# A fused attention and MoE kernel on one core: the last chunk's output in two halves, two clamps on POOL, and a new order of all operations

## Chip, cores, metric

The kernel runs on 1 core of a Trainium2 chip. The metric is the device time of one execution in microseconds. Engines: PE (matmul), DVE, ACT and POOL (elementwise work), SP (issues the DMA transfers).

## What is computed

Inputs are q, k, v of shape 4 x 8 x 768 x 64 (batch, head, position, head dimension) in f32, and two matrices, w_in (512 x 2048) and w_out (2048 x 512), in f64.

```python
k_sum = k.reshape(B, H, nb, 32, D).max(axis=3)        # 24 block summaries of k
v_sum = v.reshape(B, H, nb, 32, D).mean(axis=3)       # and of v
scores_l = scale * q @ k.T,  only where |i - j| < 16
scores_s = scale * q @ k_sum.T + log(32)
a = softmax over [scores_l, scores_s]
x = (a @ [v, v_sum]).reshape(3072, 512)
h = x @ w_in;  g = h * cos(h);  out = g @ w_out
```

## The kernel before

The 3072 rows are cut into 8 blocks of 384 rows (blk 0 to 7). Each block has two parts.

**Attention**, for four groups a, b, c, d of two heads each; a2 is group a of block 2. A group's steps: loads of q, k, v and of the summaries of v (`q k v m`, issued on SP), transposes on PE and copies into place (`tq tk cq ck`, from block 2 on `qt kt` on DVE), summaries of k (`ks`), masks and scores on PE (`ms sc`, lines 553 to 573), scores from PSUM to SBUF (`z`), maximum (`mx`, DVE), subtraction of it (`su`, POOL, line 593), exp (`ex`, ACT), sums (`sm`, DVE), reciprocal (`iv`, DVE), normalization (`nm`, POOL, line 617), transposes of the probabilities on PE and their copies (`tp cp`), the product with the values on PE (`va`, line 670), and its split into a high and a low fp32r part (`xh xl`, lines 350 and 356). `v0_0` to `v3_7` are the block sums of v (`l` load, `h` halve, `s` sum). `v0_0` holds heads 0 to 3 of batch 0, `v0_1` heads 4 to 7.

**The two products**, as 128 steps s0 to s127, each one 128-wide slice f of the 2048 columns for one block of rows. `up` (12 matmuls, line 714) gives h. `tu re si sq ga` make the gate (lines 724 to 741, ACT DVE ACT ACT DVE), `hi lo` split it (lines 350 to 356, on an engine that the order names). `dh dl` (9 matmuls, line 770) add it to three accumulators in PSUM, one for each chunk of 128 rows. At the end of a run the accumulators are copied (`ta`) and stored (`st`, SP). The runs: s0 to s5 are block 0 with slices 0 to 5, s6 to s21 block 1 with all 16, s22 to s31 block 0 with the other ten, and then one run of 16 for each of blocks 2 to 7.

**The weights** are turned from f64 words into a high and a low fp32r part on the chip, once for each slice w0 to w15: `l` (two loads of 512 KB each on SP, lines 371 and 375, into raw space that several slices share in turn; the space is given by `SLOTS`), `ab` (magnitude, ACT, line 388), `cl` (DVE, a clamp of a 128 x 1024 tile, line 393), `sh lb fb` (bits put together, DVE, lines 399 to 415), `hi` and `lo` (lines 423 and 426). s0 needs w0, s1 needs w1, and so on. So the first third of the kernel does three things at once: attention of blocks 0 and 1, the splitting of the weights, and the first steps.

Nothing in the order is decided by a scheduler: `ORDER` lists all operations as tokens, such as `w3.cl` or `s5.up.0` (the number is a PSUM bank), and every engine, SP among them, gets its own instructions in the order of that list and works through them in that order (lines 898 to 903). SP's loads go round eight semaphores; a load waits until the one eight places before it has landed. Waits between engines come from the data.

## Time and profile before

| | |
|---|---|
| median of 3 runs (lowest, highest) | 661.95 us (660.78, 662.87) |
| the profiled execution | 662.1 us |
| its span, first to last instruction | 660.2 us |
| mean granted clock of TensorE | 0.987 |
| busy: PE, DVE, ACT, POOL | 633.9, 451.1, 366.2, 214.6 us |
| moved by DMA | 72.68 MB |

In rows of the timeline the columns are start, length, engine, line, operation, output<-input, shape, count, and in brackets the idle time before and what ended it. SPq rows are issues of transfers. A window's row gives the busy time of PE, PEld, DVE, ACT and POOL with their counts, then the granted clock, the DMA engines' busy share and GB/s. A row of a group gives, behind the bar, the busy time and the mean length in ns, and then the idle time before.

### The profile page before, as it was taken

Reading aid. Unit: us, or ns where it says so; the run is one execution under the profiler, and the core shown is the slowest. Engines: PE = TensorE matmul, PEld = TensorE weight load, DVE = VectorE, ACT = ScalarE, POOL = GpSimd, SP = SyncE. Lnnn points to the kernel's source line nnn. Section 1 sums busy time; section 2 is a strip of 40 time slices with the busy share of each in tenths; the row PEclk is TensorE's granted clock in tenths of the full one; section 3 lists DMA queues with packets and bytes.
Section 4 is the critical chain, followed back from the end, with each engine's and each line's share of the span. In section 5 each row is a group of like instructions: output and inputs, shape, how many; then the busy total and the mean of one; then the engine's idle time right before and its main releaser. Section 6 shows DMA issues by size and latency. Waiting matters only on the chain.

```text
span 660.2 us, 13296 instructions
## 1 busy us (share of the span) xinstructions
PE 633.9 (96%) x5150; PEld 561.5 (85%) x5150; DVE 451.1 (68%) x792; ACT 366.2 (55%) x645; POOL 214.6 (33%) x217
## 2 busy tenths in 40 slices
PE   6569999999999999999999999999999999999997
PEld 4347889889888989898988988989898988989996
DVE  3998998988656676658786667577686564534433
ACT  3666968776663375546575663335545554443443
POOL 4674777754220242302333340012332132010001
PEclk9879999999999999999999999999999999999999
DMA  9898725443331443434553544423243424000001
GB/s 229 260 268 224 239 94 176 160 111 59 69 108 52 128 127 105 115 71 98 123 156 78 150 125 132 92 54 81 85 120 104 104 91 115 0 1 17 32 1 48
DMA packets 164647, 72.68 MB, mean 110 GB/s; under 512 B 134441, under 2 KB 153193, under 8 KB 164585
## 3 DMA queue, kind: packets, MB, share of 16 engines
q1 hardware_dynamic: 164584, 71.84, 40.6%
q8 instruction: 40, 0.66, 0.4%
q14 instruction: 23, 0.18, 0.1%
...
## 4 chain that ended last, share of the span: by engine, by line
PE 87%; SPq 4%; DMA 4%; ACT 2%; issue 1%; DVE 1%; POOL 1%; ACTq 0%
PE banks L770 40%; PE banks L714 39%; PE banks L569 4%; PE banks L670 3%; DMA late<-in_moe_w_out_dram 3%; SPq L456 1%; SPq L493 1%; SPq L477 1%; ACT stage L388 1%; ACT L732 0%; POOL w L356 0%; SPq L485 0%; PE banks L626 0%; ACT w L350 0%; SPq L254 0%
## 5 line engine op out<-in xcount | busy, mean ns | idle before, releaser
L714 PE MATMUL banks<-xh,w 128*128 128x384 f32 x1024 | 271.8, 337 | 1.1 <-ACT pt L350 0.7
L770 PE MATMUL banks<-w,gh 128*128 128x512 f32 x768 | 199.1, 394 | 0.0
L714 PEld LDWEIGHTS banks<-xh,w 128*128 128x128 f32 x1024 | 185.9, 188 | 3.9 <-ACT pt L350 0.9
L714 PE MATMUL banks<-xl,w 128*128 128x384 f32 x512 | 171.4, 335 | 0.0
L770 PEld LDWEIGHTS banks<-w,gh 128*128 128x128 f32 x768 | 142.0, 188 | 29.0
L356 POOL TENSOR_TENSOR gl<-t,gh 128x384 fp32r<-128x384 f32 x57 | 58.5, 1027 | 242.9 <-DVE gh L352 86.0
L724 ACT ACTIVATE t<-banks 128x384 int32<-128x384 f32 x128 | 62.2, 489 | 131.1 <-DVE gl L356 56.1
L727 DVE SCALAR_TENSOR_TENSOR t<-t,banks 128x384 f32<-128x384 int32 x128 | 69.5, 547 | 61.2 <-ACT t L724 60.7
L770 PE MATMUL banks<-w,gl 128*128 128x512 f32 x384 | 109.6, 393 | 0.0
L739 DVE SCALAR_TENSOR_TENSOR t<-t,banks 128x384 f32<-128x384 f32 x128 | 69.8, 547 | 45.4 <-ACT t L735 44.9
L732 ACT ACTIVATE t<-t 128x384 f32<-128x384 f32 x128 | 66.3, 523 | 60.1 <-DVE t L727 59.4
L714 PEld LDWEIGHTS banks<-xl,w 128*128 128x128 f32 x512 | 96.1, 188 | 1.7
L770 PEld LDWEIGHTS banks<-w,gl 128*128 128x128 f32 x384 | 71.3, 188 | 14.8 <-POOL gl L356 0.2
L593 POOL TENSOR_TENSOR sc<-sc,m 128x720 f32<-128x720 f32 x28 | 39.5, 1410 | 88.9 <-DVE m L588 83.8
L735 ACT ACTIVATE t<-t 128x384 f32<-128x384 f32 x128 | 65.9, 522 | 2.4
L617 POOL TENSOR_TENSOR sc<-sc,r 128x720 f32<-128x720 f32 x28 | 39.6, 1416 | 73.1 <-DVE r L614 70.2
L350 ACT CAST gh<-t 128x384 fp32r<-128x384 f32 x71 | 36.2, 510 | 41.3 <-PE banks L770 21.8
L356 DVE TENSOR_TENSOR gl<-t,gh 128x384 fp32r<-128x384 f32 x71 | 40.6, 573 | 19.6 <-PE banks L770 12.0
L356 POOL TENSOR_TENSOR w<-stage,w 128x1024 fp32r<-128x1024 f32 x15 | 36.7, 2448 | 14.7 <-ACT w L350 12.8
L569 PEld LDWEIGHTS banks<-kd,qd 64*64 64x64 f32 x1344 | 27.8, 133 | 9.6 <-issue 5.3
L580 DVE SCALAR_TENSOR_TENSOR sc<-banks,mask 128x360 f32<-128x360 f32 x48 | 24.7, 523 | 16.5 <-PE banks L569 16.3
L569 PE MATMUL banks<-kd,qd 64*64 64x96 f32 (+1 forms) x1344 | 30.9, 231 | 0.6 <-ACT qd L508 0.4
...
## 6 DMA issues: line engine op xcount, KB each, us to landing
...
```

The costliest lines, as they stand in the source:

```text
L350: eng.copy(out=out, in_=in_)
L356: eng.tensor_tensor(out=lo, in0=src, in1=hi.bitcast(F32), op=ALU.subtract)
L569: nc.tensor.matmul(out=self.sp[hh][s * QT : (s + 1) * QT, c, lo : lo + n], lhsT=self.qd[rows, t * QT : (t + 1) * QT], rhs=self.kd[rows, ke ...
L593: nc.gpsimd.tensor_tensor(out=self.sc, in0=self.sc, in1=self.m.unsqueeze(2).broadcast_to([P, U, NK]), op=ALU.subtract)
L617: nc.gpsimd.tensor_tensor(out=self.sc, in0=self.sc, in1=self.r.unsqueeze(2).broadcast_to([P, U, NK]), op=ALU.mult)
L714: nc.tensor.matmul(out=self.h, lhsT=w_of(name, self.f)[:, c * P : (c + 1) * P], rhs=x_of(self.blk, part, c), start=n == 0, stop=n == last,)
L724: nc.scalar.activation(out=self.t.bitcast(I32), in_=self.h, func=AF.Copy, scale=1.0 / TWO_PI)
L727: nc.vector.scalar_tensor_tensor(out=self.t, in0=self.t.bitcast(I32), scalar=-TWO_PI, in1=self.h, op0=ALU.mult, op1=ALU.add)
L732: nc.scalar.activation(out=self.t, in_=self.t, func=AF.Sin, scale=0.5)
L735: nc.scalar.activation(out=self.t, in_=self.t, func=AF.Square, scale=math.sqrt(2.0))
L739: nc.vector.scalar_tensor_tensor(out=self.t, in0=self.t, scalar=-1.0, in1=self.h, op0=ALU.add, op1=ALU.mult)
L770: nc.tensor.matmul(out=self.acc[i], lhsT=g[:, i * P : (i + 1) * P], rhs=w_of(name, self.f), start=self.first and n == 0, stop=self.last an ...
```

## The change

Three things are changed.

1. **The last chunk.** The third chunk of a block's last run was copied by one instruction of 512 columns and stored by one transfer of 256 KB. Now two instructions of 256 columns each copy it, on engines that the order names (`ta` and the new `tb`), and two transfers store the halves (`st` and the new `sb`). This concerns the chunk that is copied into the tile `last`, which is that of s127 only.
2. **The clamp** (`cl`) takes an engine from the order. w3 and w7 are clamped on POOL, the other 14 on DVE as before.
3. **The order.** All 2247 tokens stand in a new order, and there are two more (`s127.tb`, `s127.sb`). PSUM banks are given out differently, and some copies change their engine: of the steps' `hi`, 66 are on ACT (before 71) and 62 on DVE (57); of their `lo`, 66 on DVE (71) and 62 on POOL (57). The loads' spaces (`SLOTS`) and the runs stay.

```diff
-        def clamp(self):
+        def clamp(self, eng):
-            nc.vector.tensor_scalar(out=uf, in0=uf, scalar1=W_LO, scalar2=W_HI, op0=ALU.max, op1=ALU.min)
+            eng.tensor_scalar(out=uf, in0=uf, scalar1=W_LO, scalar2=W_HI, op0=ALU.max, op1=ALU.min)
...
-                t = xp.tile([P, 2, TB], F32R, name="last", tag="xh0%d" % (self.blk % 2))
-                self.o[i] = t.rearrange("p c n -> p (c n)")[:, :DM].bitcast(F32)
+                return self.take_half(i, 0, eng)
...
+        def take_half(self, i, h, eng):
+            if (i, 0) not in self.o:
+                t = xp.tile([P, 2, TB], F32R, name="last", tag="xh0%d" % (self.blk % 2)).rearrange("p c n -> p (c n)")
+                self.o[i, 0], self.o[i, 1] = (t[:, n * DM // 2 : (n + 1) * DM // 2].bitcast(F32) for n in range(2))
+            self.negative(eng, self.o[i, h], self.acc[i][:, h * DM // 2 : (h + 1) * DM // 2])
...
+        def store_half(self, i, h):
+            r0, c = self.blk * TB + i * P, slice(h * DM // 2, (h + 1) * DM // 2)
+            nc.sync.dma_start(out=out[r0 : r0 + P, c], in_=self.o[i, h])
...
 ORDER = """
-s127.lo.p s127.dh s127.dl s127.ta.1.1.a s127.ta.0.0.v s127.ta.2.a s127.st.1 s127.st.2 s127.st.0
+s127.lo.p s127.dh s127.dl s127.ta.2.a s127.ta.0.0.v s127.st.2 s127.tb.2.v s127.st.0 s127.ta.1.1.v s127.sb.2 s127.st.1
```

SP, from the load of w0 on (late_131 holds w0, late_125 w2, late_132 w1 and then w5; vn_103 belongs to a0, x_0_135 to c0; vs are the block sums of v, from v0_0 and v0_1). Before:

```order
L375 DMA late_131<-in_moe_w_out_dram 128x1024
L456 DMA late_130<-in_q_dram 128x3x64 x2
L477 DMA vn_103<-in_v_dram 96x5x64 x2
L485 DMA vn_103<-in_v_dram 80x2x64
L371 DMA late_125<-in_moe_w_in_dram 128x4x256
L375 DMA late_125<-in_moe_w_out_dram 128x1024
L493 DMA x_0_135<-vs_299 24x6x64 x2
L493 DMA vn_103<-vs_292 24x6x64 x2
L371 DMA late_132<-in_moe_w_in_dram 128x4x256
```

And now:

```order
L376 DMA late_131<-in_moe_w_out_dram 128x1024
L494 DMA x_0_135<-vs_297 24x6x64 x2
L372 DMA late_125<-in_moe_w_in_dram 128x4x256
L376 DMA late_125<-in_moe_w_out_dram 128x1024
L478 DMA x_0_135<-in_v_dram 96x5x64 x2
L486 DMA x_0_135<-in_v_dram 80x2x64
L494 DMA vn_103<-vs_290 24x6x64 x2
L478 DMA vn_103<-in_v_dram 96x5x64 x2
L486 DMA vn_103<-in_v_dram 80x2x64
L457 DMA late_130<-in_q_dram 128x3x64 x2
L372 DMA late_132<-in_moe_w_in_dram 128x4x256
```

The load of c1's q (late_130) has gone from the first place behind w0 to the last before w5, and the values of c0 have come ahead of a0's. Further down SP's list, w4.l stood behind a1.m, d1.m and a1.q and ahead of d0.v, c1.m, d1.q and b0.m; now it stands behind c1.m, d0.m, a1.q, d1.q, d0.v and b0.m, and ahead of b1.m, a1.m and d1.m. The loads that followed w8 in the order w7, v1_0, w9, w10, w6 (with others between) now follow as v1_0, w6, w9, w7, w10.

POOL, from w2's low part on (w_485 and w_483 are w2, w_552 and w_553 are w5; sc is a score tile of group b0 or a1). Before:

```order
L356 TENSOR_TENSOR w_485<-stage_480,w_485 128x1024
L593 TENSOR_TENSOR sc<-sc,m 128x6x120
L356 TENSOR_TENSOR w_552<-stage_520,w_552 128x1024
L617 TENSOR_TENSOR sc<-sc,r 128x6x120
L593 TENSOR_TENSOR sc<-sc,m 128x6x120
```

And now:

```order
L357 TENSOR_TENSOR w_483<-stage_465,w_483 128x1024
L594 TENSOR_TENSOR sc<-sc,m 128x6x120
L394 TENSOR_SCALAR stage_494<-stage_494 128x1024
L618 TENSOR_TENSOR sc<-sc,r 128x6x120
L594 TENSOR_TENSOR sc<-sc,m 128x6x120
L357 TENSOR_TENSOR w_553<-stage_522,w_553 128x1024
```

The clamp of w3 (L394) has come behind b0.su, and the low part of w5 has gone behind b0.nm and a1.su. The same place on DVE, with w3 as stage_501 (before) and stage_494 (now), and w4 as stage_585 and stage_587. Before:

```order
L415 SCALAR_TENSOR_TENSOR stage_520<-late_132,banks 128x1024
L393 TENSOR_SCALAR stage_501<-stage_501 128x1024
L609 TENSOR_REDUCE r<-sc 128x6
L399 TENSOR_SCALAR banks<-stage_501 128x1024
L614 RECIPROCAL r<-r 128x6
L407 SCALAR_TENSOR_TENSOR banks<-late_126,banks 128x1024
L356 TENSOR_TENSOR xl_0_588<-banks,xh_0_446 128x384
L588 TENSOR_REDUCE m<-sc 128x6
L393 TENSOR_SCALAR stage_585<-stage_585 128x1024
```

And now:

```order
L416 SCALAR_TENSOR_TENSOR stage_522<-late_132,banks 128x1024
L610 TENSOR_REDUCE r<-sc 128x6
L400 TENSOR_SCALAR banks<-stage_494 128x1024
L615 RECIPROCAL r<-r 128x6
L589 TENSOR_REDUCE m<-sc 128x6
L357 TENSOR_TENSOR xl_0_519<-banks,xh_0_500 128x384
L394 TENSOR_SCALAR stage_587<-stage_587 128x1024
L408 SCALAR_TENSOR_TENSOR banks<-late_126,banks 128x1024
```

w3's clamp is gone from DVE, a0's low part (xl_0_588 before) now stands earlier in the list than these rows, d0's low part (xl_0_519) has come ahead of w4's clamp, and w3's `lb` (L408) has gone behind it.

SP at the end of the program (stage tiles hold chunks 0 and 1, `last` chunk 2). Before:

```order
L810 DMA out_dram<-stage_6472 128x512
L810 DMA out_dram<-stage_6911 128x512
L810 DMA out_dram<-last 128x512
L810 DMA out_dram<-stage_6913 128x512
L929 UNCONDITIONAL_BRANCH
```

And now:

```order
L827 DMA out_dram<-stage_6552 128x512
L831 DMA out_dram<-last 128x256
L827 DMA out_dram<-stage_6915 128x512
L831 DMA out_dram<-last 128x256
L827 DMA out_dram<-stage_6920 128x512
L954 UNCONDITIONAL_BRANCH
```

The first row is an earlier block's store. Of s127's stores, chunk 1 was first, chunk 2 second and chunk 0 last; now they are the first half of chunk 2, chunk 0, the second half of chunk 2, chunk 1. On ACT the copies of chunks 1 and 2 are replaced by that of the first half; DVE copies chunk 0, the second half and then chunk 1.

319 lines of the change are left out of this document (166 added, 153 removed).

## The prediction

> **What bounds the kernel now.** I read the page first, then the busy time in windows, then the timeline of PE.
>
> ```profile
> PE 633.9 (96%) x5150; PEld 561.5 (85%) x5150; DVE 451.1 (68%) x792; ACT 366.2 (55%) x645; POOL 214.6 (33%) x217
> 80.00:90.00 10.00, 9.32 (x70) 7.84 (x69) 9.79 (x15) 9.78 (x17) 7.94 (x8) 1.00 0.17 45
> 300.00:400.00 100.00, 100.00 (x957) 88.79 (x956) 74.23 (x141) 63.05 (x103) 35.36 (x33) 1.00 0.49 122
> ```
>
> PE is busy 633.9 of 660.2 us, so 26.3 us are all that any order of the same matmuls could win. From 84 us to the last matmul there is no gap (the window 300:400 is full, at clock 1.00). What can move is therefore the first 84 us and the end. The rows of PE that matter at the start:
>
> ```profile
> 48.33 1.26 PE L670 MATMUL banks<-pt,x 120*64 120x64 f32 x24 [2.17 <-DMA x<-in_v_dram]
> 58.27 0.43 PE L714 MATMUL banks<-xh,w 128*128 128x384 f32 x1
> 66.94 1.09 PE L626 MATMUL banks<-ident,late 128*120 128x128 f32 x6 [0.49 <-POOL late L617]
> 68.42 0.44 PE L714 MATMUL banks<-xh,w 128*128 128x384 f32 x1 [0.39 <-ACT late L350]
> 83.15 0.44 PE L714 MATMUL banks<-xh,w 128*128 128x384 f32 x1 [0.68 <-ACT pt L350]
> 94.45 4.19 PE banks L714 x24
> ```
>
> 58.27 is s0.up, the first matmul of the two products, and needs the last x part of block 0 (b0.xl, on DVE). 94.45 (from the chain) is s6.up, where the first run is done. Between the two PE waits only 0.49 + 0.39 + 0.68 = 1.56 us. Before s0.up DVE is the limit:
>
> ```profile
> 17.16 1.38 DVE L259 TENSOR_TENSOR late<-late 96x1024 f32<-96x1024 f32 x1 [1.16 <-DMA late<-in_v_dram]
> 22.61 1.65 DVE L393 TENSOR_SCALAR stage<-stage 128x1024 f32<-128x1024 f32 x1 [0.37 <-ACT stage L388]
> 24.19 0.18 DVE L614 RECIPROCAL r<-r 128x6 f32<-128x6 f32 x1
> 44.73 0.72 DVE L393 TENSOR_SCALAR stage<-stage 128x1024 f32<-128x1024 f32 x1
> 45.78 0.91 DVE L609 TENSOR_REDUCE r<-sc 128x6 f32<-128x726 f32 x1 [0.32 <-ACT sc L606]
> 49.00 0.55 DVE L356 TENSOR_TENSOR xl<-banks,xh 128x384 fp32r<-128x384 f32 x1
> 51.17 1.26 DVE L393 TENSOR_SCALAR stage<-stage 128x1024 f32<-128x1024 f32 x1 [0.82 <-ACT stage L388]
> 57.57 0.56 DVE L356 TENSOR_TENSOR xl<-banks,xh 128x384 fp32r<-128x384 f32 x1
> ```
>
> In order: the halving of v0_0, w1.cl, a0.iv, w3.cl, b0.sm, a0.xl, w4.cl, b0.xl. From w1.cl on DVE runs almost without a break to b0.xl, which ends at 58.13, and s0.up follows 0.14 us later.
>
> **The start, term by term.** Every instruction up to s0.up is the same but for w3.cl, which goes to POOL.
>
> First, up to b0.sm. a0.sm and a0.iv go ahead: a0.sm now runs in the 1.16 us that DVE waits for v0_0, and a0.iv no longer stands behind w1.cl (0.18 us off that stretch). w1.cl itself took 1.65 us where w3.cl took 0.72; the difference is POOL's work beside it:
>
> ```profile
> 21.71 0.24 POOL L280 TENSOR_SCALAR vs<-vs 96x64 f32<-96x64 f32 x1
> 22.33 1.39 POOL L593 TENSOR_TENSOR late<-late,m 128x720 f32<-128x720 f32 x1 [0.39 <-DVE m L588]
> L297 POOL TENSOR_SCALAR_AFFINE_SELECT mask<-mask 64x384 f32<-64x384 f32 x2 | 1.0, 524 | 0.1
> L259 POOL TENSOR_TENSOR late<-late 96x1024 f32<-96x1024 f32 x1 | 2.4, 2353 | 0.0
> 44.94 0.81 ACT L606 ACTIVATE sc<-sc 128x720 f32<-128x720 f32 x1 [0.96 <-POOL sc L593]
> ```
>
> c0.su ends at 23.72, and w1.cl can only then go. With c0.mx earlier, c0.su starts when POOL is free, at 21.95, 0.4 us sooner; I take 0.3. So DVE is about 0.5 us ahead when it comes to b0.sm. w3.cl's 0.72 us ahead of b0.sm also goes, but the earlier a0.xl (0.55 us) takes most of its place, and b0.sm waits for b0.ex anyway (0.32 us now). b0.sm: 0.6 us earlier, at about 45.2.
>
> Then w3.sh, behind b0.sm, now waits for POOL's clamp. POOL can start it when b0.su is done, as ACT starts b0.ex; so it has b0.ex (0.81 us) and b0.sm (0.91 us), 1.7 us, before DVE waits. The trace has no clamp of this size on POOL. The nearest one-input row, 524 ns for 384 elements, gives 1024/384 × 0.524 = 1.4 us; the two-input row of 1024 elements gives 2.35 us. I take 1.4 (one input, like the clamp): no wait. At 2.35 it is 0.65 us. The Trainium skill, page "GPSIMD Engine Reference", section 3.1, puts a light one-input body at 1.03 cycles an element against some 2.5 for two inputs, which at its 1.2 GHz would be 0.9 us, an estimate from that page; by it the sum is that with no wait, by the two-input row the sum is 0.65 us more. No run yet shows it.
>
> From b0.sm to b0.xl. Before: 45.78 to 58.13, 12.35 us. Now a0.xl is out of it (0.5 us), and the wait of 0.82 us for w4.ab changes. ACT did w4.ab at 50.01, behind d0.xh, which waited for d0.va, which waited 2.17 us for d0.v. The loads of d0.v came behind w4.l and now stand ahead of it. What then comes last is w4's own load:
>
> ```profile
> 41.64 5.98 DMA late<-in_moe_w_out_dram
> 56.41 6.92 DMA late<-in_moe_w_out_dram
> 50.01 1.14 ACT L388 ACTIVATE stage<-late 128x1024 f32<-128x1024 f32 x1
> 17.58 3.30 SPq L456 DMA_DIRECT2D late<-in_q_dram  x2
> 71.51 1.14 ACT L388 ACTIVATE stage<-late 128x1024 f32<-128x1024 f32 x1 [0.74 <-DMA late<-in_moe_w_out_dram]
> ```
>
> w4 landed 5.98 us after its issue, at 47.62. Five more issues stand ahead of it now (c1.m, d1.q, d0.v and b0.m against a1.m and d1.m), at about 0.8 us each 4 us; against that SP's slow issues between 17 and 27 us fall away in part (c1.q alone took 3.30 us for two), since SP then waits for v0_1 with less in flight. I take the difference as 1 us, so w4 lands at 48.6 and w4.ab ends at 49.8, against 51.15. w4.cl then may meet a1.su on POOL as it met it before (1.26 us, not 0.72). From w4.cl's end to b0.xl's end DVE has the same work but for d0.xl, done before, against w3.lb, done after. I take 1.1 us less than the 12.35: the 0.5 of a0.xl and 0.6 of the wait.
>
> Start: 0.6 + 1.1 = **1.7 us earlier at s0.up** (56.6). Bounds: 0, if w4 lands 7 us after a later issue; 2.6, if DVE nowhere waits.
>
> Second, s0.up to s6.up, 36.18 us now. c1.nm goes ahead of b1.su, so the 0.49 us at 66.94 and the 0.39 at 68.42 should go; s4.up goes ahead of s0.dh, so PE reaches d1.tp with more done. But d1.nm on POOL now stands behind v1_0.s:
>
> ```profile
> 77.45 1.39 POOL L617 TENSOR_TENSOR late<-late,r 128x720 f32<-128x720 f32 x1
> 81.66 1.26 POOL L259 TENSOR_TENSOR kn<-kn 96x256 f32<-96x256 f32 x2
> 83.00 0.32 POOL L275 TENSOR_TENSOR vs<-kn 96x64 f32<-96x64 f32 x1
> ```
>
> That is 1.26 + 0.32 = 1.58 us ahead of a step that PE will want sooner, so a wait at d1.tp of up to 1.6 us takes the place of the others. w7.cl on POOL frees 0.7 us of DVE in a window where DVE has 9.79 of 10 us full, at 1.4 us of POOL behind d1.nm, where w7.sh is due some 3 us later: no cost. Of the 1.56 us I take **0.3 us** as won; bounds 1.6 lost, 1.5 won.
>
> **The middle, 94 to 650 us.**
>
> ```profile
> 183.84 8.20 PE banks L770 x36
> L739 DVE SCALAR_TENSOR_TENSOR t<-t,banks 128x384 f32<-128x384 f32 x128 | 69.8, 547 | 45.4 <-ACT t L735 44.9
> ```
>
> PE never waits there before. An up is 12 matmuls, 2.1 us (4.19 for 24), a step's downs are 9, 2.05 us (8.20 for 36). Counted so in the order, PE has at least 6.2 us of other matmuls between an up and its down before (s33), and 5.8 now (s5). In that time stand six instructions on ACT and DVE, none much longer than the gate's 0.55 us: 3 to 4 us. I cost the middle at nothing; without that cover each lack is a wait of its size, 0.4 us for s5 if it was just enough before.
>
> **The end.**
>
> ```profile
> 655.18 0.69 DVE L805 TENSOR_SCALAR stage<-banks 128x512 f32<-128x512 f32 x1 [2.07 <-PE banks L770]
> 655.40 0.60 ACT L803 ACTIVATE stage<-banks 128x512 f32<-128x512 f32 x1 [3.35 <-PE banks L770]
> 656.03 0.33 SPq L810 DMA_DIRECT2D out_dram<-stage  x1
> 656.08 0.60 ACT L803 ACTIVATE last<-banks 128x512 f32<-128x512 f32 x1
> 656.71 0.33 SPq L810 DMA_DIRECT2D out_dram<-last  x1
> 657.13 0.41 SPq L810 DMA_DIRECT2D out_dram<-stage  x1
> 656.50:657.00 0.50, 0.00 (x0) 0.00 (x0) 0.00 (x0) 0.18 (x1) 0.00 (x0) 1.00 0.25 94
> 658.50:659.00 0.50, 0.00 (x0) 0.00 (x0) 0.00 (x0) 0.00 (x0) 0.00 (x0) 1.00 0.79 303
> ```
>
> Here the first store leaves at 656.03, while the last chunk's copy still runs, and the 786 KB of the three stores then move from about 656.9 (0.25 of the first window) to 658.9 (0.79 of the last): 2.0 us, bound by the transfer. In the new order the first store on SP is the first half of the *last* chunk, and the two whole chunks, ready at 655.9 and later, queue behind it. Its copy is halved: 256 columns, between half of 0.60 and all of it, and I take 0.37 us, done at 656.45. First issue 656.48 instead of 656.03: **0.45 us later**, and the same bytes follow; the four issues (0.33 to 0.41 us each, last at about 657.7) keep ahead of the data. Bounds: 0.3 and 0.8 us, if the pieces of 1 KB a row move slower or the last issue runs dry. Chunk 1's copy, now on DVE behind both others, ends at about 657.1 and hides behind those issues.
>
> **Sum.** The profiled execution took 662.1 us for a span of 660.2, and is 0.15 us above the median of the three runs (661.95). −1.7 − 0.3 + 0.45 = −1.55: 660.55 against 662.1, which is **660.4 us** against the median.
>
> **Rivals.** *All covers hold.* DVE finds w4.cl ready (0.82 us and 0.54 us of its 1.26 more) and PE the other 1.2 us of its 1.56: −1.7 − 0.9 − 1.5 + 0.45 − 0.15 = 658.3 at best, 658.8 as its likely value. For it: the waits have single causes, and their causes have moved ahead. Against: DVE's 9.79 of 10.
>
> *The start wins nothing.* Either w4 lands 7 us after an issue at 43.3, like the load at 56.41, so that w4.ab ends at 51.4, as before; or POOL's two new clamps hold DVE's fast copies, as c0.su held w1.cl by 0.93 us. The tail stays: 662.1 + 0.45 − 0.15 = 662.4. The Trainium skill, "GPSIMD Engine Reference", section 8, says that GpSimd shares its SBUF interfaces with VectorE and collides with two-port instructions; the row at 22.61 agrees with it.
>
> *Slower: w9's load.* w6.l now stands ahead of w9.l on SP and waits for w4.fb on DVE; behind it SP is blocked. w9.ab stands on ACT ahead of s2.tu, d1.ex and s2.si. Before, w9.ab already waited 0.74 us for its load at 71.51. In the new order I want it at about 70, with the issue near 60.5 and a landing near 67.5. Each microsecond past 70 goes to PE. At 72 the 2.0 us of the start are gone, from 73.5 the kernel is slower; at 74.5 the time is 662.1 + 0.45 + 2.5 − 0.15 = 664.9. For it: the 1 MB of w6 before it. Against: it is issued 3 us sooner than before.
>
> **How the numbers follow.** A measurement of this kernel can tell about 0.3% from no change: 2.0 us, so below 659.96 is faster, above 663.94 slower. Forecast 0.46 (its own range 659.4 to 661.6; 0.13 of it below 659.96), all covers hold 0.24, the start wins nothing 0.17, slower 0.13. Faster 0.24 + 0.13 = 0.37, slower 0.13, same 0.50. The range 658.2 to 662.9 leaves out the slower case and about 0.06 of the fast one.
>
> **What would show it.** s0.up at 56.6 (59 would refute the first term); POOL's clamp at 1.4 us and w3.sh directly behind b0.sm; PE's wait at d1.tp for POOL; s6.up at about 92.5; no PE wait after it; the first output store issued at 0.4 us after the last matmul ends. A PE wait of over 1 us anywhere past 95 us, or w9.ab idle for its load, makes the forecast wrong.

## The result, and the profile after

The changed kernel takes 665.99 us (median of 6 runs, 664.87 to 667.85), the kernel before 662.41 us (6 runs, 660.78 to 663.10): 1.0051 times as long, 95% interval 1.0032 to 1.0069. It is slower by 3.4 us, where the forecast had 1.5 us less and a range that ended at 662.9. The profiled execution took 667.05 us for a span of 665.2 us.

First the rows of the start on all engines, in order of time; in the timeline of before b0.sm stood at 45.78, s0.up at 58.27.

```profile
32.49 0.50 SPq L376 DMA_DIRECT2D late<-in_moe_w_out_dram  x1
38.09 1.13 ACT L389 ACTIVATE stage<-late 128x1024 f32<-128x1024 f32 x1 [2.78 <-DMA x<-vs]
39.25 0.69 DVE L394 TENSOR_SCALAR stage<-stage 128x1024 f32<-128x1024 f32 x1 [1.85 <-ACT stage L389]
45.59 0.49 SPq L376 DMA_DIRECT2D late<-in_moe_w_out_dram  x1
45.93 3.61 POOL L394 TENSOR_SCALAR stage<-stage 128x1024 f32<-128x1024 f32 x1
46.83 0.91 DVE L610 TENSOR_REDUCE r<-sc 128x6 f32<-128x726 f32 x1 [0.63 <-ACT sc L607]
49.58 1.23 DVE L400 TENSOR_SCALAR banks<-stage 128x1024 int32<-128x1024 int32 x1 [1.84 <-POOL stage L394]
51.05 1.39 POOL L618 TENSOR_TENSOR sc<-sc,r 128x720 f32<-128x720 f32 x1 [1.50 <-DVE r L615]
51.83 1.14 ACT L389 ACTIVATE stage<-late 128x1024 f32<-128x1024 f32 x1 [2.60 <-DMA late<-in_moe_w_out_dram]
52.49 0.70 PE L627 MATMUL banks<-ident,sc 128*120 128x128 f32 x4 [3.47 <-POOL sc L618]
59.86 0.44 PE L715 MATMUL banks<-xh,w 128*128 128x384 f32 x1 [0.15 <-DVE xl L357]
```

In order: the second load of w5 goes out at 32.49 (30.71 before), and w5.ab at 38.09 waits for it. The releaser that its row names is a transfer into x, which w5.ab does not read; what it reads is w5's raw words. w5.cl on DVE waits 1.85 us for w5.ab. The second load of w4 goes out at 45.59 (41.64 before) and w4.ab at 51.83 waits 2.60 us for it. POOL's clamp of w3 takes 3.61 us, w3.sh on DVE waits 1.84 us for it, b0.iv stands behind w3.sh, so b0.nm on POOL starts only at 51.05 (49.07 before) and PE's transposes of b0 wait 3.47 us. The load is not all that holds w4.ab: it writes the stage space that w3.sh reads (`w3.ab.0` and `w4.ab.0` name the same one), and w3.sh ends at 50.81, so only the last 1.0 of its 2.60 us are the load's alone. s0.up starts at 59.86, 1.6 us later than before and 3.3 us later than forecast.

From s0.up to s6.up the profile has some 38.6 us where before had 36.0 (the instants are in the table below). PE's waits in it:

```profile
69.86 0.52 PE L503 MATMUL banks<-ident,qn 128*128 128x128 f32 x3 [1.24 <-ACT t L733]
80.20 0.73 PE L771 MATMUL banks<-w,gh 128*128 128x512 f32 x2 [1.34 <-DVE qd L353]
85.38 0.43 PE L627 MATMUL banks<-ident,late 128*120 128x128 f32 x2 [1.16 <-DVE t L740]
96.34 0.96 PE L771 MATMUL banks<-w,gl 128*128 128x512 f32 x3 [0.31 <-DVE gl L357]
```

They sum to 4.05 us and are new ones: a2.tq finds its PSUM bank 1 taken, s0.dh finds bank 1 still held by a2.tq until DVE has copied it, d1.tp finds bank 7 held by s3.up. After 98 us PE waits once more, 0.35 us at 124.88.

The tail: the last matmul, the three copies of chunk 2's halves and chunk 1, and the first and last of SP's four issues.

```profile
659.94 0.39 PE L771 MATMUL banks<-w,gl 128*128 128x512 f32 x1
660.37 0.38 ACT L807 ACTIVATE last<-banks 128x256 f32<-128x256 f32 x1 [2.79 <-PE banks L771]
660.78 0.42 DVE L809 TENSOR_SCALAR last<-banks 128x256 f32<-128x256 f32 x1 [0.63 <-ACT last L807]
661.12 0.68 DVE L809 TENSOR_SCALAR stage<-banks 128x512 f32<-128x512 f32 x1
660.77 0.33 SPq L831 DMA_DIRECT2D out_dram<-last  x1
662.17 0.39 SPq L827 DMA_DIRECT2D out_dram<-stage  x1
```

The two halves run one behind the other, not side by side. The first issue starts 0.44 us after the last matmul's end (0.02 us before it in the kernel before), the last issue ends 2.23 us after it (1.49 before), and the span ends 4.87 us after it (4.15 before).

One profile is one execution, and the runs of one kernel differ by 2 to 6 us here. So here are the same four instants from the profiles of all kernels but pool_forms (s0.tu and s6.tu are ACT's first step behind s0.up and s6.up; what the names stand for is told below):

| kernel | s0.tu | s6.tu | last matmul ends | span ends |
|---|---|---|---|---|
| before | 60.65 | 96.64 | 656.05 | 660.2 |
| b_w3_pool | 60.56 | 97.04 | 656.43 | 660.6 |
| b_stores_012 | 61.62 | 96.46 | 656.70 | 660.7 |
| b_w7_pool | 61.40 | 101.90 | 661.48 | 665.6 |
| b_w7_again | 60.71 | 98.58 | 657.84 | 662.0 |
| b_w7_fill | 60.78 | 99.58 | 658.83 | 663.0 |
| b_clamps_pool | 60.99 | 100.33 | 659.61 | 663.8 |
| b_sp_after | 65.26 | 100.14 | 659.47 | 663.6 |
| after | 62.26 | 100.83 | 660.33 | 665.2 |
| a_old_tail | 63.74 | 99.06 | 658.51 | 662.6 |
| a_st0_first | 64.06 | 100.43 | 659.17 | 663.6 |
| a_two_tiles | 62.30 | 98.68 | 657.45 | 662.4 |
| a_banks | 63.30 | 99.68 | 658.48 | 663.4 |
| a_w4_early | 62.55 | 100.04 | 658.78 | 663.7 |
| a_c0m_behind | 62.67 | 99.04 | 658.39 | 663.3 |
| a_clamps_dve | 62.94 | 99.74 | 658.51 | 663.4 |
| a_sp_before | 62.09 | 99.16 | 659.21 | 664.1 |
| a_sp_clamps | 62.65 | 98.30 | 657.08 | 662.0 |
| a_three_undone | 64.15 | 100.66 | 659.39 | 663.5 |

From s6.tu to the last matmul every row has 558.7 to 560.2 us. Apart from these 1.5 us, what a kernel loses or wins is decided before s6.tu, at about 100 us, and in the tail. The four profiles with the start of the changed kernel untouched (after, a_old_tail, a_st0_first, a_two_tiles) differ among themselves by 1.8 us at s0.tu and by 2.2 us at s6.tu. b_stores_012, which is the kernel before up to its last 5 us, has s0.tu 1.0 us later than before has. So a single profile shows mechanisms, and a difference of 1 or 2 us between two of them shows nothing by itself.

### The profile page after: what moved, and what is told of

Same layout as the page of the kernel before. It is cut to its first block, busy times and chain, and to the rows that moved or that the text cites. A ratio compares the mean times of both kernels' runs of the same rounds, so it can differ in the third digit from the quotient of the medians.

```text
span 665.2 us, 13298 instructions
## 1 busy us (share of the span) xinstructions
PE 633.8 (95%) x5150; PEld 561.8 (84%) x5150; DVE 451.9 (68%) x789; ACT 364.9 (55%) x640; POOL 229.6 (35%) x230
## 4 chain that ended last, share of the span: by engine, by line
PE 82%; DVE 5%; DMA 5%; SPq 4%; ACT 1%; issue 1%; POOL 1%; DVEq 0%; ACTq 0%; POOLq 0%
PE banks L771 37%; PE banks L715 36%; PE banks L570 4%; DMA late<-in_moe_w_out_dram 3%; PE banks L671 3%; SPq L457 1%; DMA late<-in_q_dram 1%; SPq L494 1%; DVE banks L400 1%; DVE banks L408 1%; DVE stage L416 1%; SPq L478 1%; DVE stage L394 1%; ACT stage L389 1%; DVE t L740 1%
## 5 line engine op out<-in xcount | busy, mean ns | idle before, releaser
L771 PEld LDWEIGHTS banks<-w,gh 128*128 128x128 f32 x768 | 142.5, 188 | 30.4 <-DVE qd L353 1.8
L357 POOL TENSOR_TENSOR gl<-t,gh 128x384 fp32r<-128x384 f32 x62 | 62.8, 1014 | 240.9 <-PE banks L771 86.5
L351 ACT CAST gh<-t 128x384 fp32r<-128x384 f32 x66 | 33.7, 510 | 45.5 <-PE banks L771 28.6
L353 DVE CAST gh<-t 128x384 fp32r<-128x384 f32 x62 | 24.2, 391 | 11.6 <-PE banks L771 9.8
(103 smaller groups left out, 628.0 us busy)
```

The source lines that it names most:

```text
L351: eng.copy(out=out, in_=in_)
L357: eng.tensor_tensor(out=lo, in0=src, in1=hi.bitcast(F32), op=ALU.subtract)
L771: nc.tensor.matmul(out=self.acc[i], lhsT=g[:, i * P : (i + 1) * P], rhs=w_of(name, self.f), start=self.first and n == 0, stop=self.last an ...
```

## The experiments

Names that begin with a_ are the changed kernel with something undone or moved, names with b_ the kernel before with one thing done. Times are ratios to the kernel before on the same chip, with the 95% interval.

### Parts of the change undone, one at a time

**a_clamps_dve**: the two clamps back on DVE.

```diff
-w3.cl.p ... w7.cl.p
+w3.cl.v ... w7.cl.v
```

> The changed kernel (665.99 us) with the clamps of w3 and w7 back on DVE, nothing else. Theory: the new order lost 4.2 us up to s6.up in three places: two clamps of 3.6 us on POOL, loads issued 2 to 4 us later on SP, and PSUM banks that PE finds taken at 69 to 86 us; the tail lost 0.7 us more. By it the clamp of w3 (1.84 us of wait at w3.sh) and the late load of w4 (2.60 us of wait at w4.ab) lie side by side, so that taking the clamp away alone wins only about 0.6 us at s0.up (59.86 to 59.3), and w7's clamp another 0.3 to 0.5: 665.0 us. Rival 1: the clamps are the whole loss of the start and, through b0.nm and b1.nm behind them on POOL, of the stretch after it: 662 to 663 us, with s0.up at 58.0. Rival 2: the clamps cost nothing, for DVE is spared as much: 666 us.

Measured: 665.8 us, 1.0044 (1.0026 to 1.0062). The clamps alone are not the loss: rival 1 falls. It is 0.07% less than the changed kernel's 1.0051. The interval holds both the theory's gain of 1 us and rival 2, nothing.

**a_sp_before**: SP's order from c1.q to w8.l as before. The rows are SP's tokens.

```diff
-c0.m w2.l c0.v a0.m a0.v c1.q w5.l b1.q c1.m w3.l d0.m a1.q d1.q d0.v b0.m w4.l b1.m a1.m d1.m b0.v a1.v b1.v c1.v w8.l
+c1.q a0.v w2.l c0.m a0.m w5.l c0.v d0.m b1.q w3.l a1.m d1.m a1.q w4.l d0.v c1.m d1.q b0.m c1.v b0.v a1.v w8.l b1.m b1.v
```

> The changed kernel with SP's loads from c1.q to w8.l in the order of the kernel before (c1.q and a0.v ahead of c0.m; w5.l ahead of c0.v; w4.l ahead of d0.v, c1.m, d1.q and b0.m), all other engines as changed. Theory: w5.ab no longer waits 2.78 us for its load, so DVE has not its 1.85 us of idle time at w5.cl, and w4.ab not its 2.60 us; s0.up comes about 1.9 us earlier (58.0) and the time is 664.1 us; the wait of w3.sh for POOL's clamp stays at about 1.8 us. Rival 1 (the clamps alone hold the start): s0.up stays within 0.4 us of 59.86 and the time at 666 us, the wait at w3.sh growing by what the loads give. Rival 2: the loads win the 1.9 us but PE gives them back before s6.up to the banks or to DVE: s0.up 58.0, s6.up 98.5, 666 us.

Measured: 664.07 us, 1.0030 (1.0015 to 1.0045), as the theory had it in time. Not in its instant: s0.up comes at 59.70 instead of the 58.0 expected, and s0.tu at 62.09 is 0.2 to 2.0 us earlier than in the four profiles with the untouched start. The profiled execution took 666.04 us, 2.0 us more than the median, so it does not show where the time is won. It shows two things at work. ACT's w4.ab no longer waits for a load, though it starts no sooner than in the changed kernel (51.83), and DVE still waits for POOL's clamp:

```profile
49.41 1.23 DVE L400 TENSOR_SCALAR banks<-stage 128x1024 int32<-128x1024 int32 x1 [1.21 <-POOL stage L394]
51.93 1.15 ACT L389 ACTIVATE stage<-late 128x1024 f32<-128x1024 f32 x1
```

**a_banks**: the two PSUM banks on which PE waited are freed earlier.

```diff
-PE:  ... s1.up.6 a1.va.2 c1.tp.0.3 a2.tq.1 c1.tp.1.0 ... s0.dh.5.6.1 s0.dl s1.dh ...
+PE:  ... s1.up.6 a1.va.2 c1.tp.0.3 c1.tp.1.0 ... s0.dh.5.6.1 s0.dl a2.tq.0 s1.dh ...
-DVE: ... c1.xh.v a2.cq.v s3.re d1.sm c1.xl d1.iv a1.xl s2.ga s2.hi.v w9.sh.2.3 s3.ga ...
+DVE: ... c1.xh.v s3.re d1.sm c1.xl d1.iv a1.xl a2.cq.v s2.ga s2.hi.v s3.ga w9.sh.2.3 ...
```

> The changed kernel with three steps moved: a2.tq behind s0.dl on PE and in bank 0 instead of bank 1, with a2.cq behind it on DVE, and s3.ga ahead of w9.sh on DVE; all else as changed. PE's three waits of 1.24 us at 69.86 (d1.z.1 on ACT holds bank 1), 1.34 us at 80.20 (a2.cq on DVE holds bank 1 for s0.dh) and 1.16 us at 85.38 (s3.ga on DVE holds bank 7 for d1.tp) lose their cause. Theory: most of them go, s6.up comes 1.5 to 3 us earlier than 98.66 and the time is 663.5 us (663 to 664.5). Rival: DVE is what bounds 80 to 110 us (9.7 of 10 us busy), so the waits come back elsewhere, at the downs or at s6.up; s6.up moves by less than 0.5 us and the time stays at 665.5 to 666 us.

Measured: 666.81 us, 1.0057 (1.0037 to 1.0077). In its profile the three waits are gone, and the time is not less; the rival holds. In the profile of a_old_tail, with the same start as the changed kernel, PE waits 1.2 us between s0.up and s6.up instead of 4.05. So the bank waits look like slack: s6.tu comes at 98.7 to 100.8 us with and without them.

**a_old_tail**: the tail of before.

```diff
-s127.ta.2.a s127.ta.0.0.v s127.st.2 s127.tb.2.v s127.st.0 s127.ta.1.1.v s127.sb.2 s127.st.1
+s127.ta.1.1.a s127.ta.0.0.v s127.ta.2.a s127.st.1 s127.st.2 s127.st.0
```

> The changed kernel with the tail of the kernel before: chunk 1 copied whole on ACT, chunk 0 on DVE, chunk 2 whole on ACT, three stores in the order 1, 2, 0; the rest as changed. Theory: the tail from the last matmul's end to the span's end goes from 4.86 us back to about 4.15 us: 665.3 us. Rival 1: the tail's 0.7 us are no more than what one profile differs from another, and the time stays at 666.0 us. Rival 2 (the tail as I first had it, 0.45 us): 665.5 us.

Measured: 665.93 us, 1.0050 (1.0033 to 1.0068): the time cannot show 0.7 us here. The profiles do: 4.09 us from the last matmul to the span's end, against 4.87 with the new tail. This is the steadiest difference of all: the nine profiles with the tail of before have 4.1 to 4.2 us, the seven others with the new one 4.9 to 5.0.

**a_sp_clamps**: both start edits undone, the diffs of a_clamps_dve and a_sp_before together.

> The changed kernel with both start edits undone at once: SP's loads from c1.q to w8.l in the order of the kernel before, and the clamps of w3 and w7 on DVE. Alone, the loads gave 1.9 us (664.07 against 665.96, the changed kernel and its twin with the old tail together) and the clamps 0.2 us, which the time cannot tell from nothing. Theory: the late loads hid the clamps' price; with the loads early the 1.8 us that w3.sh waits for POOL is last, so the two together give more than the sum, about 3.3 us: 662.6 us, with s0.up at 58.3 to 58.8. Rival: the clamps cost nothing in either order, since DVE is spared 0.7 us each and waits elsewhere: 664.0 us.

Measured: 663.35 us, 1.0018 (1.0010 to 1.0026), between the two. Going back from a_sp_before to this, the clamps are worth about 0.8 us, where alone they were worth 0.5 (the intervals overlap). In the profile s0.tu still comes at 62.65, 2.0 us later than in that of before.

**a_three_undone**: the same with the tail of before; what is left of the change is the order of PE, ACT, DVE and POOL, and SP's behind w8.l.

> The changed kernel with three things undone: the clamps of w3 and w7 on DVE, SP's loads from c1.q to w8.l in the order of before, and the tail of before. What is left of the change is the new order of PE, ACT, DVE and POOL. With the first two undone it took 1.0018 times the kernel before, 1.2 us more, of which the tail's 0.75 us go here. Theory: the rest of the order is worth nothing: 662.4 us, within 0.5 us of the kernel before. Rival 1 (my forecast for the order alone): it is worth 2.0 us once the clamps, the loads and the tail are out of it: 660.2 us. Rival 2: the order itself still costs 1 us or more (its PSUM banks): 663.3 us.

Measured: 663.49 us, 1.0006 (0.9992 to 1.0021). The theory fits: the rest of the order is worth something between 0.5 us won and 1.4 us lost. Rival 1, my own forecast, would need 0.997 and is outside the interval; rival 2, a loss of 1 us (1.0017), is inside it. That the loss of the changed kernel lies in the three things together is shown, for its interval (from 1.0032) and this one (to 1.0021) do not meet. The ladder 1.0051, 1.0030, 1.0018, 1.0006 gives 1.4 us to the loads, 0.8 to the clamps and 0.8 to the tail, but each rung's interval is about as wide as the rung, so this split is an estimate. The profiled execution (665.33 us, 1.8 above the median) has s0.tu at 64.15: it does not show the start won back.

### Parts of the change done alone, in the kernel before

**b_clamps_pool**: both clamps on POOL, at their old places. **b_w7_pool** and **b_w3_pool**: one each.

```diff
-w3.cl ... w7.cl
+w3.cl.p ... w7.cl.p
```

> The kernel before (662.6 us over all its runs) with the clamps of w3 and w7 on POOL, at the places in the order where they stand, nothing else. Theory: POOL starts w3's clamp behind b0.su, takes 3.6 us, and w3.sh on DVE waits 1.5 to 2 us for it, of which 0.7 us is spared by the clamp that DVE no longer does; b0.nm on POOL comes 2 us later, and PE's transposes of b0 wait: s0.up 1 to 1.5 us later (59.5), 663.9 us. Rival: the clamps alone change nothing: 662.6 us.

> The kernel before (662.2 us) with only w7's clamp on POOL. With both clamps on POOL it took 665.9 us, and in that profile s0.up was 0.3 us later than before, but PE waited 3.00 us at 85.27 (0.68 us before) and TensorE's granted clock fell to 0.50 behind that wait, so that s5.up's matmuls took 0.52 us where they took 0.34. Theory: w7's clamp is the loss: POOL is 3.6 us in it, s2's low part stands behind it, s4.tu on ACT waits for that, and the clock takes another 1.3 us: 665.2 us, s6.up 3 us later than 94.45 or more. Rival: both clamps cost about the same, 1.9 us each: 664.0 us.

> The kernel before (662.2 us) with only w3's clamp on POOL. Theory (the loss of both is w7's): w3.sh on DVE waits 1.85 us for POOL, but DVE is spared 0.7 us and w4.ab's load is the later wait; s0.up 0.3 to 0.5 us later than 58.27 and 662.6 us. Rival: both clamps cost the same, 664.0 us, with s0.up 1.5 us later or a lower clock in its stretch.

Measured: both 1.0063 (1.0038 to 1.0087), w7's alone 1.0054 (1.0032 to 1.0075), w3's alone 0.9998 (0.9985 to 1.0011). For both, the expectation (663.9 us) put the loss in the wrong clamp and was too low. The split is clear: in this order w3's costs nothing and w7's is all of it, 3.6 us. Yet in the profile of b_w3_pool w3.sh waits for POOL as long as in the changed kernel:

```profile
48.65 1.23 DVE L399 TENSOR_SCALAR banks<-stage 128x1024 int32<-128x1024 int32 x1 [1.84 <-POOL stage L393]
```

So that wait alone need not cost anything at s0.up. The profile of b_w7_pool shows how w7's clamp costs its time, on POOL, ACT and PE:

```profile
81.52 3.62 POOL L393 TENSOR_SCALAR stage<-stage 128x1024 f32<-128x1024 f32 x1 [1.02 <-ACT stage L388]
85.11 0.99 POOL L356 TENSOR_TENSOR gl<-t,gh 128x384 fp32r<-128x384 f32 x1
86.13 0.49 ACT L724 ACTIVATE t<-banks 128x384 int32<-128x384 f32 x1 [2.19 <-POOL gl L356]
86.52 0.37 ACT L350 COPY pt<-banks 120x256 f32<-120x256 f32 x1
86.94 0.69 PE L714 MATMUL banks<-xh,w 128*128 128x384 f32 x1 [3.18 <-ACT pt L350]
```

s2.lo stands behind the clamp on POOL, s4.tu on ACT waits for it, d1's copy stands behind s4.tu, and s5.up waits for the bank that the copy frees. In the changed kernel w7's clamp stands behind s2.lo, not ahead of it (83.88 and 84.85 in its timeline of POOL), and that chain does not arise: the same 3.6 us, one place later, cost PE nothing that the profile shows.

**b_sp_after**: SP's order of the changed kernel in the kernel before (d1.v behind w9.l too).

```diff
-c1.q a0.v w2.l c0.m a0.m w5.l c0.v d0.m b1.q w3.l a1.m d1.m a1.q w4.l d0.v c1.m d1.q d1.v b0.m c1.v b0.v a1.v w8.l
+c0.m w2.l c0.v a0.m a0.v c1.q w5.l b1.q c1.m w3.l d0.m a1.q d1.q d0.v b0.m w4.l b1.m a1.m d1.m b0.v a1.v b1.v c1.v w8.l
```

> The kernel before with SP's loads from c1.q to w8.l (and d1.v behind w9.l) in the order of the changed kernel, all else as before. Theory: c0.m at the head of the queue holds SP for v0_1's sums, w5.l and w4.l go out 2 to 4 us later, and w5.ab and w4.ab on ACT wait for their loads as in the changed kernel: 1.9 us slower, 664.5 us. Rival: the loads only cost time together with the changed order of the computing engines, which asks for w5 and w4 earlier: 662.6 to 663.0 us.

Measured: 664.39 us, 1.0033 (1.0017 to 1.0049), as the theory said, and the rival falls. The load order costs about 2 us in either order of the computing engines. In the profile w5.ab waits 2.42 us and w4.ab 2.10 us for their loads, as the theory has it, but PE also waits 7.10 us at 34.34 for a0's values (4.89 us at the same place before), which the theory did not name; s0.tu comes 4.6 us later than before.

### The loads taken apart

**a_w4_early** moves one load, **a_c0m_behind** two (SP's tokens):

```diff
-... a1.q d1.q d0.v b0.m w4.l ...
+... a1.q w4.l d1.q d0.v b0.m ...
```

```diff
-... c0.m w2.l c0.v a0.m a0.v c1.q w5.l ...
+... c1.q a0.v c0.m w2.l c0.v a0.m w5.l ...
```

> The changed kernel (1.0050 of the kernel before) with w4.l on SP ahead of d1.q, d0.v and b0.m instead of behind them, nothing else. With the whole stretch of loads in the old order it is 1.0030. Theory A: w4's late load is the cost (w4.ab waits 2.60 us for it): 1.0032, s0.up 1.5 us earlier. Theory B: the cost comes earlier, from SP's stall at c0.m and the late w5: 1.0048, for the clamp of w3 and b0.nm behind it hold b0 anyway, and w4.ab's wait is only slack.

> The changed kernel with c1.q and a0.v ahead of c0.m on SP (c1.q, a0.v, c0.m, w2.l, c0.v, a0.m, then w5.l as now), nothing else. SP no longer stands still from 19.2 to 22.05 us. Theory B (the stall and the late w5 are the cost of the load order): w5.l goes out about 2 us earlier, w5.ab's wait of 2.78 us and DVE's 1.85 us at w5.cl shrink to under 1 us, 1.0035. Theory A (w4's load): 1.0048.

Measured: 1.0074 (1.0047 to 1.0100) and 1.0053 (1.0034 to 1.0072). Neither load alone brings anything back, so both theories fall as put. In the profile of a_c0m_behind w5.ab no longer waits for its load, but b0 is held by the clamp as before:

```profile
49.27 1.23 DVE L400 TENSOR_SCALAR banks<-stage 128x1024 int32<-128x1024 int32 x1 [1.84 <-POOL stage L394]
52.17 1.11 PE L627 MATMUL banks<-ident,sc 128*120 128x128 f32 x4 [3.25 <-POOL sc L618]
```

For w4 the profiles show why one undoing is not enough: two waits lie side by side at w4.ab. With its load early (a_w4_early) it waits for w3.sh, and so for POOL's clamp; with the clamps on DVE (a_clamps_dve) it waits for the load. First a_w4_early, then a_clamps_dve:

```profile
51.49 1.13 ACT L389 ACTIVATE stage<-late 128x1024 f32<-128x1024 f32 x1 [0.92 <-DVE banks L400]
51.26 1.16 ACT L389 ACTIVATE stage<-late 128x1024 f32<-128x1024 f32 x1 [1.76 <-DMA late<-in_moe_w_out_dram]
```

With both undone (a_sp_clamps) it starts at 51.41 even so, now behind d0.xh, for which ACT waits 1.11 us on PE. Which loads make up the 1.4 to 2.2 us of the whole stretch stays open.

### What a clamp takes on POOL

**pool_forms**: five later clamps of the kernel before on POOL, in four forms. w11 leaves the upper bound out.

```diff
+            if self.f == 11:
+                eng.tensor_scalar_max(uf, uf, W_LO)
+            elif self.f == 15:
+                eng.tensor_scalar_max(uf, uf, W_LO)
+                eng.tensor_scalar_min(uf, uf, W_HI)
+            elif self.f == 14:
+                for h in range(2):
+                    u = uf[:, h * DM : (h + 1) * DM]
+                    eng.tensor_scalar(out=u, in0=u, scalar1=W_LO, scalar2=W_HI, op0=ALU.max, op1=ALU.min)
```

> One look at what POOL needs for a clamp of 128x1024 f32: the kernel before with five later clamps on POOL (w12 and w13 as in the change; w11 with the lower bound only, which leaves the upper bound out; w15 as two instructions of one bound each; w14 as two instructions of 512 columns with both bounds). Theory 1: the two operations of a column stand one behind the other (a chain of two), about 3.5 ns a column: with one operation an instruction takes 1 to 1.5 us, so w15's two 2 to 3 us, less than the 3.62 us of one instruction with both; w14's halves 1.8 to 1.9 us each. Theory 2: the price is per column whatever is done: one operation takes 3.6 us as well.

The groups by line: 403 is w12 and w13, 401 w14's halves, 396 and 397 w15's two instructions, 394 w11.

```profile
L403 POOL TENSOR_SCALAR stage<-stage 128x1024 f32<-128x1024 f32 x2 | 7.3, 3628 | 0.1
L401 POOL TENSOR_SCALAR stage<-stage 128x512 f32<-128x512 f32 x2 | 3.8, 1918 | 0.6 <-ACT stage L388 0.6
L396 POOL TENSOR_SCALAR stage<-stage 128x1024 f32<-128x1024 f32 x1 | 3.0, 2957 | 0.2 <-ACT stage L388 0.2
L394 POOL TENSOR_SCALAR stage<-stage 128x1024 f32<-128x1024 f32 x1 | 2.8, 2776 | 0.0
L397 POOL TENSOR_SCALAR stage<-stage 128x1024 f32<-128x1024 f32 x1 | 2.8, 2775 | 0.1
```

Neither theory: one bound alone takes 2.78 us (2.96 in one of the three), both in one instruction 3.63 us, so the second operation costs about 0.85 us and the first, with what every column costs, 2.78. From the halves: 3.63 less 1.92 us for 512 columns is 3.3 ns a column and 0.2 us for an instruction. (The kernel ran once, 675.79 us; only these lengths are read from it.)

### How much of it is TensorE's clock

In the profile of b_w7_pool the granted clock falls to 0.50 behind the wait of 3.18 us, and s5.up's matmuls then take 0.52 us. **b_w7_fill** puts 14 transposes of the identity into that wait, into PSUM columns that nothing reads; **b_w7_again** is b_w7_pool once more, beside it.

```diff
-... d1.tp.1.0 s5.up.0 ...
+... d1.tp.1.0 f.fl.4.14 s5.up.0 ...
+    class Filler:
+        def fill(self, i, n):
+            for _ in range(n):
+                nc.tensor.transpose(out=bank(i)[:, TB : TB + P], in_=ident, identity=ident)
```

> The kernel before with w7's clamp on POOL, and 14 transposes of the identity (some 2.4 us of PE, into columns of a PSUM bank that nothing reads) right ahead of s5.up, where PE would else wait 3.18 us. Theory: the wait costs time twice, by its length and by the clock behind it; with PE busy the granted clock stays at 1.00 there, s5.up to s6.up takes 11.3 us as before instead of 12.6, and the time is 1.3 us less than the twin's: about 1.0035 of the kernel before against 1.0054. Rival: the clock's fall costs nothing, since PE waits for DVE behind it anyway: the same time as the twin.

> The kernel before with w7's clamp alone on POOL, once more: 1.0054 of the kernel before (1.0032 to 1.0075), PE's wait of about 3 us ahead of s5.up, and the granted clock at 0.50 behind it.

Measured: 1.0035 (1.0021 to 1.0048) with the filling, 1.0051 (1.0034 to 1.0069) without. That is 1.1 us, near the 1.3 us that the theory gave to the clock, but the intervals overlap. In the profile of b_w7_fill the transposes take 1.69 us, PE still waits 1.65 us behind them, and the granted clock is 1.00 throughout; but so it is in that of b_w7_again, so this one profile does not show that the filling kept it there. The profiles of the one program, b_w7_pool and b_w7_again, show it better. Of b_w7_pool the second matmul of s5.up and the window behind it, with the granted clock as the third number from the end:

```profile
87.43 0.52 PE L714 MATMUL banks<-xl,w 128*128 128x384 f32 x1
88.00:90.00 2.00, 2.00 (x8) 2.00 (x8) 1.97 (x3) 1.96 (x3) 2.00 (x2) 0.50 0.28 92
```

and of b_w7_again the first two, and the window:

```profile
85.10 0.44 PE L714 MATMUL banks<-xh,w 128*128 128x384 f32 x1 [3.20 <-ACT pt L350]
85.38 0.34 PE L714 MATMUL banks<-xl,w 128*128 128x384 f32 x1
86.00:88.00 2.00, 2.00 (x29) 1.75 (x29) 1.97 (x3) 1.96 (x3) 2.00 (x2) 1.00 0.29 89
```

The same program, the same wait (3.18 and 3.20 us), and the matmul behind it takes 0.52 us in one execution and 0.34 in the other. The executions took 667.44 and 663.80 us. From the wait's end to s6.tu they need 14.96 and 13.48 us (b_w7_fill 13.49), and PE waits for nothing else in between: 1.5 us of the difference is the clock's.

### The tail

**a_st0_first** stores chunk 0 first, **b_stores_012** stores in the order of the copies in the kernel before, **a_two_tiles** gives each half of chunk 2 an SBUF tile of its own.

```diff
-s127.ta.0.0.v s127.st.2 s127.tb.2.v s127.st.0 ...
+s127.ta.0.0.v s127.st.0 s127.st.2 s127.tb.2.v ...
```

```diff
-s127.ta.1.1.a s127.ta.0.0.v s127.ta.2.a s127.st.1 s127.st.2 s127.st.0
+s127.ta.0.0.v s127.ta.1.1.a s127.ta.2.a s127.st.0 s127.st.1 s127.st.2
```

```diff
-            if (i, 0) not in self.o:
-                t = xp.tile([P, 2, TB], F32R, name="last", tag="xh0%d" % (self.blk % 2)).rearrange("p c n -> p (c n)")
-                self.o[i, 0], self.o[i, 1] = (t[:, n * DM // 2 : (n + 1) * DM // 2].bitcast(F32) for n in range(2))
+            t = xp.tile([P, 2, TB], F32R, name=f"last{h}", tag="x%s0%d" % ("hl"[h], self.blk % 2))
+            self.o[i, h] = t.rearrange("p c n -> p (c n)")[:, : DM // 2].bitcast(F32)
```

> The changed kernel with one step moved: chunk 0's store ahead of the first half of chunk 2 on SP. In four profiles with the new tail 4.86 to 4.92 us lie between the last matmul's end and the span's end, in two with the old tail 4.09 to 4.15. Theory: what counts is when SP's last issue ends, four issues of 0.4 us of which the first starts 0.44 us after the last matmul; with chunk 0 first that one is done by then, and the last issue waits only for chunk 1's copy (about 0.3 us earlier): the tail is 4.5 us. Rival: the pieces of 1 KB a row move slower, and the tail stays at 4.86 us whatever goes first. The time itself (665.6 us) cannot tell these apart.

> The kernel before with the three last stores in the order of their chunks' copies, 0, 1, 2 instead of 1, 2, 0, the copies as before. In four tails the span ended 2.6 us after SP's last issue ended (before: last matmul 656.05, last issue to 657.54, span 660.2; changed: 660.33, 662.56, 665.2; chunk 0 first: 659.17, 661.00, 663.6). Theory: the last issue's end sets the tail: here the last issue needs chunk 2's copy and ends about 1.05 us after the last matmul instead of 1.49, so the tail is 3.7 us instead of 4.15, and the time 0.4 us less, 0.9993. Rival: the transfer itself bounds the tail (786 KB in 2.0 us), and with the same first issue it stays at 4.1 us.

> One look: the changed kernel with the two halves of the last chunk in two tiles of SBUF instead of one. Theory 1: the wait of DVE's half for ACT's half (0.63 us) comes from the PSUM bank that both read, and stays. Theory 2: it comes from the shared tile, and goes: DVE's half starts with ACT's, 0.4 us earlier, and chunk 1's copy behind it too. The tail is set by SP's four issues and shrinks by 0.1 us at most in either case.

Measured: a_st0_first 1.0049 (1.0030 to 1.0067), its tail 4.43 us, as the theory had it (4.5). The last matmul of b_stores_012 and its last issue:

```profile
656.31 0.39 PE L770 MATMUL banks<-w,gl 128*128 128x512 f32 x1
657.45 0.41 SPq L810 DMA_DIRECT2D out_dram<-last  x1
```

The issue ends 1.16 us after the last matmul (656.70), 0.33 us sooner than before, but the tail is 4.0 us, only 0.15 less: between theory and rival. From the last issue's end to the span's end there are 2.6 us in after, a_st0_first and before, and 2.84 here, where the three issues are early: here something else, probably the transfer, begins to bound the tail. The time, 1.0018 (1.0002 to 1.0033), went up for a kernel that differs from before in its last 5 us alone and is not slower there. So even an interval that leaves out 1 by so little is no proof of an effect here.

a_two_tiles ran once, 664.19 us: DVE's half waits as in the changed kernel.

```profile
657.90 0.42 DVE L809 TENSOR_SCALAR last<-banks 128x256 f32<-128x256 f32 x1 [0.63 <-ACT last L807]
```

So it is not the tile; what the halves still share is the PSUM bank, and that it is the bank is argued, not shown. Copies out of two banks do overlap on DVE and ACT (655.18 and 655.40 before). The Trainium skill, "PSUM — Partial Sum Buffer", section "PSUM bank collisions raise a hardware error", says that the compiler's scheduler puts a dependency between any two instructions of different engines on one bank and the same 32 partitions, reads alike; the 0.63 us agree with a rule of that kind.

## Why the prediction was wrong

**First term, s0.up 1.7 us earlier, 56.6: failed.** It came at 59.86, and "59 would refute the first term" was the text's own bound. In the four profiles with this start it comes at 59.9 to 61.7, in five with the start of before at 58.2 to 59.0. In the sum's own terms, b0.sm was to come 0.6 us earlier and came 1.05 us later (46.83), and the stretch from b0.sm to b0.xl was to lose 1.1 us and grew by 0.6 (b0.xl ends at 59.81). Three steps failed, two for a price or a time that I took from the wrong row, one because the sum does not have it.

- *"I take 1.4 (one input, like the clamp)".* It is 3.62 us, beyond the upper bound of 2.35. The way of reckoning was right: 3.61 us less the cover of 1.72 is a wait of 1.9 us at w3.sh, and 1.84 was measured. The price was not: I scaled the affine select and bounded it by the two-input row. The prediction quoted the same operation on POOL: the TENSOR_SCALAR of 96x64 at 21.71, 0.24 us for 64 columns. Scaled by 16 that is 3.8 us, and it was the only row with two operations on one input. That it comes so near is in part luck, for by the 3.3 ns a column and 0.2 us an instruction that are found above, 64 columns would take 0.4 us. The Trainium skill's figure ("GPSIMD Engine Reference", section 3.1, 1.03 cycles an element for a light body) gave an estimate of 0.9 us; by measurement it does not hold for this instruction. Left out were the two ways on which the wait is passed on: b0.iv stands behind w3.sh on DVE, so b0.nm and PE wait, and w4.ab waits for the space that w3.sh reads.
- *"I take the difference as 1 us, so w4 lands at 48.6 and w4.ab ends at 49.8".* w4's second load went out at 45.59 and w4.ab ended at 52.97. The issues added ahead of it were counted, but SP's standing still at c0.m (19.2 to 22.1 us in its timeline) was named and given no length; I had written that SP's slow issues "fall away in part". The rival "the start wins nothing" had this price, at a chance of 0.17, and even it was too mild: the start was lost, not only not won. In two of the four profiles with this start, a_st0_first and a_two_tiles, w4.ab's row names w3.sh and not the load, so the load is only one of two waits that end together there.
- *The load of w5 has no term.* It went out 1.8 us later, w5.ab waited for it, and w5.cl starts at 39.25 instead of 38.07. Behind w5.cl stand w2.fb, w2's two parts and, on POOL, b0.su (44.57, before 43.51), and behind that b0.ex and b0.sm: this is the 1.05 us.

What these steps are worth in time is known only from the experiments: about 2 us for the loads' order, 0.5 to 0.8 us for both clamps, with w3's alone worth nothing in the order of before. In no profile does undoing them bring s0.tu back to that of before (62.65 in a_sp_clamps, 64.15 in a_three_undone, against 60.65), so by which way the loads' 2 us reach the end stays open.

**Second term, 0.3 us won from s0.up to s6.up: not seen, and inside its bounds.** From s0.tu to s6.tu the four profiles with the untouched start have 38.57, 35.32, 36.37 and 36.38 us, before 35.99 and b_stores_012, with the same start as before, 34.84: on average a loss of 1.2 us, which so few profiles cannot tell from nothing. The wait I named (d1.tp behind v1_0.s on POOL) did not come, d1.tp waited 1.16 us for DVE instead; waits for PSUM banks came, which I had not looked for, and a_banks shows that they cost nothing that the time can tell. "w7.cl: no cost" held in the new order, where it stands behind s2.lo; b_w7_pool shows that one place earlier it costs 3.6 us, so the text was right without having shown why.

**Middle, nothing: right, within what the profiles can tell.** 558.7 to 560.2 us from s6.tu to the last matmul in all profiles, and before and b_stores_012, which are the same there, differ by 0.8; one wait of 0.35 us at 124.88.

**End, 0.45 us later: the mechanism half right, the size too small, 0.7 us (bounds 0.3 to 0.8).** The first issue is 0.46 us later against the last matmul, as forecast. "The same bytes follow; the four issues keep ahead of the data" failed: the data stream is not full from its start. Two windows of before, where it is, and two of after:

```profile
657.00:657.50 0.50, 0.00 (x0) 0.00 (x0) 0.00 (x0) 0.00 (x0) 0.00 (x0) 1.00 1.04 385
657.50:658.00 0.50, 0.00 (x0) 0.00 (x0) 0.00 (x0) 0.00 (x0) 0.00 (x0) 1.00 1.03 393
661.50:662.00 0.50, 0.00 (x0) 0.00 (x0) 0.31 (x1) 0.00 (x0) 0.00 (x0) 1.00 0.72 254
662.00:662.50 0.50, 0.00 (x0) 0.00 (x0) 0.00 (x0) 0.00 (x0) 0.00 (x0) 1.00 0.81 295
```

The fourth issue ends 0.74 us later against the last matmul than the third did.

**Sum.** s0.tu is later by 1.6 to 3.4 us in the four profiles with the untouched start than in that of before, not earlier by 1.7; the stretch to s6.tu gives between a loss of 2.6 and a gain of 0.7; the tail costs 0.7. The measured loss is 3.4 us. The slower rival (w9's load late) came true as a sign, for w9.ab waited 1.97 us for it at 74.80, and its 664.9 us for such a time is the figure of the text nearest to the result. It did not decide: in the other three profiles with this start w9.ab waits for no load, and undoing the clamps, the loads up to w8.l and the tail, with w9.l left where the change put it, brings 1.0006.

**What the prediction gave no term** is TensorE's clock, though it is the smaller part. In half-microsecond windows up to 135 us I add PE's idle time and its busy time times (1 − granted clock). That lost time is 27.3 us before, 32.8 after, 33.5 in b_w7_pool and 30.4 in b_w7_again; the last matmul's end less it is 628.8, 627.5, 628.0 and 627.4 us. Over all kernels of the table this remainder is 625.9 to 628.8 us (b_w7_fill, which has 14 matmuls more, 630.2), so the account closes to 3 us. Within that, the differences between kernels, and between two executions of one kernel, are PE's lost time in the start. Of the 5.5 us between before and after, 4.4 are idle time (22.1 and 26.5 us) and 1.1 the clock (5.2 and 6.3 us). The clock's part changes as much between executions: it is 7.6 us in b_stores_012, which has the start of before. The Trainium skill, "TensorE: Matmul & The Clock Gate", Part 1, has the clock at half after an idle window of about 3.4 us, with windows that run free of the program. That they run free would explain why the same wait is followed by half clock in one execution and not in the other. But the wait of 3.18 us is shorter than such a window, and waits of 1.57 us (a_sp_before, at 70.04) were also followed by 0.56, which the rule with a whole idle window does not give by itself.
